# Sparse attention and a two-layer network on one core: plain chunks unit by unit with the gate in two steps, weight sums made in place, and another order of the up phase

## The chip, the cores and the metric

The program runs on one core of one Trainium2 chip. Its time is the device time of one execution in microseconds. Five engines run their own instruction queues in order and wait for one another at semaphores: TensorE (PE in the profile, its weight loads PEld), VectorE (DVE), ScalarE (ACT), GpSimd (POOL) and SyncE (SP), which issues the DMAs.

## What is computed

Attention over 8 batches, 8 heads, 576 positions with 64 elements a head; four heads see the last 32 positions, four see every 32nd. The result, as 4608 tokens of 512 elements, goes through a layer of 2048, a gate and a layer of 512, all in float32:

```python
scores = np.where(masks, scale * q @ k.T, -1e9)
attn = np.exp(scores - scores.max(-1)); attn /= attn.sum(-1) + 1e-09
x = (attn @ v).transpose(0, 2, 1, 3).reshape(4608, 512)
h = x @ w_in
g = np.where(h >= 1, h, np.where(h <= -1, 0.0, (h + 1) ** 2 / 4))
return g @ w_out
```

## The kernel before

Every product of float32 matrices is made of three fp32r matmuls, high by high, high by low and low by high, so each operand is split into a rounded high part (ACT) and the rest (DVE). The tokens go through in stages:

- **Head**: attention of batch 0.
- **Plain chunks** c = 0, 1, 2 of 512 tokens. A chunk has 16 units f of 128 hidden elements. `up(c, f)` makes h with 12 matmuls; `gate` (L620) makes the gate: `bent` and `squared` on ACT, `gated` on DVE, then the high part gh (ACT, L631; DVE in chunk 0) and the rest gl (DVE, L634); `down` (L640) adds the unit to four output banks with 12 matmuls. h has two PSUM banks in turn. In chunk 0 `down` takes one unit at a time, two units behind `up`; in chunks 1 and 2 two units at once, as soon as three are pending.
- **Super-chunks** s = 0, 1, 2 of 1024 tokens, by a Strassen scheme with 7 products in place of 8. In the up phase, `up_block` (L708), 8 pairs j of units run through 7 products m each, in the order of `UP` (L662), with 6 matmuls a product. Three accumulators belong to a pair: Y takes products 1, 6, 7 and 4, X takes 2, Z takes 5 and 3. Between the products ACT copies a bank out before the next product is added to it, DVE adds banks together, and the four gates of a pair are made. Then comes the down phase, `down_block`, with 56 products over the split gates `hl` (`prep`, L783).

The factors of the Strassen products are read from DRAM, seven ahead, into a ring of tiles (`fetch_w`). They are written there in chunks 1 and 2: `ship` (L231) writes the weights as they are, and for each of the 2 times 8 pairs a block of four **weight sums**. These are made by POOL in `recall` (L241: two adds of 512 elements, high plus low of the weights) and `combine` (L246: four adds or subtractions of 256), then split by ACT and DVE in `ship_sums` (L255) and written to DRAM as 1 MB. The attention of batches 2 to 7 runs in small steps beside all this: `START` and `LATER` give the quarter unit g at which each step stands, so its place is fixed against the products of PE. POOL also makes two steps of each softmax (L412, L436).

The order is written out by hand (`manual_schedule`); each engine works in the order of the program. h in `COMBINE` (L924) counts half units. For an entry at h, `recall` stands at h − 1, `combine` at h and `ship_sums` at h + 1, and the entries are 3 apart. All sums of chunk 1 use one room for the recalled weights and one for the sums, both in the tile xs_0 that later takes attention outputs; those of chunk 2 use rooms in w0 and w1. The outputs of a chunk leave through three `ob` buffers that attention uses as well (L652).

Of the kernel before, what the change touches and what calls it, by code (L numbers as in the profile page):

```python
# [17 lines left out]
P = 128  # L18
EPS = 1e-09
ST = 32  # L20
WR = 7
# [4 lines left out]
def tile_sparse_attention_then_ffn(  # L26
# [214 lines left out]
    def recall(i, j, w32):  # L241
        for f in range(2):
            hi, lo = (wt[2 * j + f][:, i, :, x].bitcast(F32) for x in range(2))
            nc.gpsimd.tensor_tensor(out=w32[:, 2 * f:2 * f + 2], in0=hi, in1=lo, op=ALU.add)

    def combine(i, j, w32, st):  # L246
        def block(r, c):
            return w32[:, 2 * r + c if i == 0 else 2 * c + r]

        s_ = [st[:, n, HF:] for n in range(4)]  # L250
        for to, a, b, op in ((0, block(1, 0), block(1, 1), ALU.add), (1, s_[0], block(0, 0), ALU.subtract),
                             (2, block(0, 0), block(1, 0), ALU.subtract), (3, block(0, 1), s_[1], ALU.subtract)):
            nc.gpsimd.tensor_tensor(out=s_[to], in0=a, in1=b, op=op)  # L253
# [366 lines left out]
    def gate(c, f, between=lambda: None):  # L620

        hp = o_ps.pop((c, f))
        u, gh, gl = (short(n, d, f"{a}_{c}_{f}") for n, d, a in ((6, F32, "u"), (f % 3, F32R, "gh"), (3 + f % 3, F32R, "gl")))
        bent(u, hp)
        squared(u)
        between()

        g = u if (c, f) == (0, 0) else hp
        gated(g, hp, u)
        if c:  # L630
            nc.scalar.copy(gh, g)  # L631
        else:
            nc.vector.tensor_copy(gh, g)
        nc.vector.tensor_tensor(out=gl, in0=g, in1=gh.bitcast(F32), op=ALU.subtract)  # L634
        return gh, gl
# [4 lines left out]
    def down(*units):  # L640

        c, f0, f1 = units[0][0], units[0][1], units[-1][1]
        if f0 == 0:
            o_ps[c] = [psum("o", [P, CH], f"o_{c}_{d}") for d in range(NC)]
        for d in range(NC):
            h, e = divmod(d * P, HF)
            for _, f, gs in units:
                for n, (x, y) in enumerate(HI_LO):
                    nc.tensor.matmul(o_ps[c][d], wt[f][:, 1, h, x, e:e + P], gs[y],  # L649
                                     start=f == 0 and n == 0, stop=f == NF - 1 and n == 2)  # L650
            if f1 == NF - 1:
                ob = o_p.tile([P, CH], F32, tag="ob", name=f"ob_{c}_{d}")  # L652
# [8 lines left out]
    FACTOR = {1: (0, 0), 2: (0, 1), 4: (0, 2), 5: (1, 0), 6: (1, 1), 7: (1, 2), 3: (1, 3)}  # L661
    UP = [(j - late, m) for j in range(NP + 1) for m, late in ((1, 0), (2, 0), (3, 1), (6, 0), (4, 1), (5, 0), (7, 0)) if 0 <= j - late < NP]  # L662
# [45 lines left out]
    def up_block(s, between):  # L708
        y, x, z = {}, {}, {}
        room = slot(TMP, [P, 4, CH], F32, f"tmp_{s}")  # L710
        tmp = [room[:, 2 * j % 4:2 * j % 4 + 2] for j in range(NP)]
        sets = (("b2", "b0", "b1"), ("b3", "b4", "b5"))
        for n, (j, m) in enumerate(UP):
            w_ = factor(0, j, m)
            k, jj = divmod(j, 2)
            at = sets[jj]
            if m == 1:
                y[j] = bank(at[0], [P, CH], f"y_{s}_{j}")
# [5 lines left out]
            elif m == 2:  # L724
                x[j] = bank(at[1], [P, CH], f"x_{s}_{j}")
            elif m == 5:
                z[j] = bank(at[2], [P, CH], f"z_{s}_{j}")
# [7 lines left out]
            g11, g12, g21, g22 = ga[k][:, 0, jj], ga[k][:, 1, jj], gb[k][:, 0, jj], gb[k][:, 1, jj]  # L735
            ua, ub = (tmp[j][:, i] for i in range(2))
            if m == 1:
                last = (gb[(j - 1) // 2][:, 1, (j - 1) % 2], tmp[j - 1][:, 1]) if j else None
                if last:
                    bent(last[1], last[0])  # L740
                nc.scalar.copy(g11, y[j])  # L741
                if last:
                    squared(last[1])
                    gated(last[0], *last)
            elif m == 2:
                nc.vector.tensor_tensor(out=g11, in0=x.pop(j), in1=g11, op=ALU.add)
                bent(ua, g11)
                squared(ua)
            elif m == 3:
                nc.vector.tensor_tensor(out=g12, in0=z.pop(j), in1=g12, op=ALU.add)  # L750
                bent(ub, g12)
            elif m == 6:
                nc.scalar.copy(g12, y[j])
                gated(g11, g11, ua)
                if j:
                    last = ga[(j - 1) // 2][:, 1, (j - 1) % 2], tmp[j - 1][:, 1]
                    squared(last[1])
                    gated(last[0], *last)
            elif m == 4:
                h = y.pop(j)  # L760
                bent(ua, h)
                squared(ua)
                gated(g21, h, ua)
                if jj:
                    nc.gpsimd.tensor_tensor(out=ga[k][:, 1], in0=gb[k][:, 1], in1=ga[k][:, 1], op=ALU.subtract)  # L765
            elif m == 5:
                nc.scalar.copy(g22, z[j])  # L767
            elif m == 7:
                nc.vector.tensor_tensor(out=g22, in0=y[j], in1=g22, op=ALU.add)
                if j == NP - 1:  # L770
                    bent(ub, g22)
                    squared(ub)
                    gated(g22, g22, ub)
            if j == NP - 1 and m == 3:
                squared(ub)
# [289 lines left out]
```

## Time and profile before

| | |
|---|---|
| time, median of 3 runs | 923.0 us (921.79 to 925.13) |
| the profiled execution | 923.32 us, of which 921.5 us are the span |
| PE busy | 840.6 us, 91%; mean granted clock 0.968 |
| DVE, ACT, POOL busy | 560.0, 493.9, 241.7 us |
| HBM read and written | 147.26 and 46.66 MB |

The stages in the time of the profile: head to 26.5 us, chunk 0 to 118.8, chunk 1 to about 260, chunk 2 to 393.5, then up and down phases that begin at 393.5 and 500.6 (s = 0), 588.7 and 677.3 (s = 1), 761.7 and 838.2 (s = 2). "Idle before" beside an instruction is the time in which its engine waited in front of it, and the arrow names what ended the wait. A busy engine of a stage is to be read against the stage's length, and the granted clock beside it tells whether PE's matmuls ran at full speed.

### The profile page before, as it was taken

What the parts mean: (1) busy time and instruction counts of PE and PEld (TensorE: products, weight loads), DVE (VectorE), ACT (ScalarE), POOL (GpSimd) and SP (SyncE); (2) the same over time, 40 slices, a digit from 0 to 9 for tenths busy, and PEclk for the clock granted to TensorE, in tenths of its full rate; (3) what the DMA queues carried; (4) which work ended last, traced back from release to release, by engine and by line L of the source; (5) the groups of instructions that cost most, each with busy time, mean ns of one, the idle gap of its engine ahead of it and who ended that gap; (6) DMA issues with size and microseconds to landing.
All of it is one profiled execution on the core that took longest, in us unless ns stands there. A gap on an engine that the chain in (4) does not pass through costs nothing.

```text
span 921.5 us, 17868 instructions
## 1 busy us (share of the span) xinstructions
PE 840.6 (91%) x6965; PEld 669.2 (73%) x6965; DVE 560.0 (61%) x822; ACT 493.9 (54%) x852; POOL 241.7 (26%) x244
## 2 busy tenths in 40 slices
PE   8999989859979878859999998999999899999997
PEld 6788867647768756647877786777878678887886
DVE  6899835535434453555676778567567773456665
ACT  5888833334353343436766455357764435776442
POOL 6454336646215556111223000023110000111000
PEclk9999998978989989979999999999999999999999
DMA  9908136745664765558788775678766576666664
GB/s 355 408 26 309 57 112 226 268 159 192 223 210 139 263 229 171 189 189 281 226 279 282 216 238 181 212 248 232 229 179 213 163 222 209 194 194 182 210 195 159
DMA packets 105251, 195.10 MB, mean 212 GB/s; under 512 B 17104, under 2 KB 32464, under 8 KB 104272
## 3 DMA queue, kind: packets, MB, share of 16 engines
q1 hardware_dynamic: 105168, 193.96, 65.4%
q8 instruction: 55, 0.90, 0.4%
q14 instruction: 28, 0.23, 0.1%
HBM read 147.26 MB, written 46.66 MB: 210 GB/s over the span
## 4 chain that ended last, share of the span: by engine, by line
PE 51%; DVE 20%; ACT 15%; DMA 6%; issue 4%; POOL 4%; SPq 1%; ACTq 0%; DVEq 0%; POOLq 0%
PE o L649 10%; PE y L731 9%; PE h L608 8%; PE yo L837 8%; DVE hl L700 5%; PE z L731 4%; PE xo L837 4%; ACT hl L699 3%; PE xp L509 3%; ACT tmp L612 2%; PE x L731 2%; ACT tmp L615 2%; PE sc L346 2%; POOL xs L253 2%; DVE pr L397 1%
## 5 line engine op out<-in xcount | busy, mean ns | idle before, releaser
L731 PE MATMUL y<-x,wr 128*128 128x512 f32 x576 | 144.9, 397 | 12.9 <-ACT ga L741 8.9
L649 PE MATMUL o<-gh,w 128*128 128x512 f32 x384 | 133.2, 414 | 21.7 <-ACT gh L631 21.7
L608 PE MATMUL h<-xq,w 128*128 128x512 f32 x576 | 145.5, 403 | 0.8 <-DVE xq L572 0.5
L837 PE MATMUL yo<-hl,wr 128*128 128x512 f32 x576 | 135.8, 392 | 6.5 <-DVE hl L700 5.7
L731 PEld LDWEIGHTS y<-x,wr 128*128 128x128 f32 x576 | 107.2, 189 | 39.9 <-ACT ga L741 9.3
L837 PEld LDWEIGHTS yo<-hl,wr 128*128 128x128 f32 x576 | 107.3, 188 | 33.1 <-DVE hl L700 9.2
L608 PEld LDWEIGHTS h<-xq,w 128*128 128x128 f32 x576 | 109.7, 194 | 26.2 <-DVE xq L572 1.2
L649 PEld LDWEIGHTS o<-gh,w 128*128 128x128 f32 x384 | 76.4, 199 | 40.5 <-ACT gh L631 23.8
L412 POOL TENSOR_TENSOR pr<-pr,st 128x768 f32<-128x768 f32 (+3 forms) x31 | 38.2, 1233 | 176.2 <-DVE st L408 176.0
L649 PE MATMUL o<-gl,w 128*128 128x512 f32 x192 | 79.0, 411 | 0.3 <-DVE gl L634 0.2
L837 PE MATMUL zo<-hl,wr 128*128 128x512 f32 x288 | 69.1, 394 | 7.4 <-DVE hl L700 4.5
L731 PE MATMUL z<-x,wr 128*128 128x512 f32 x288 | 74.3, 393 | 1.1 <-ACT gab L767 1.1
L837 PEld LDWEIGHTS zo<-hl,wr 128*128 128x128 f32 x288 | 53.5, 188 | 22.4 <-DVE hl L700 7.0
L436 POOL TENSOR_TENSOR pr<-pr,st 128x648 f32<-128x648 f32 (+3 forms) x30 | 35.8, 1195 | 127.2 <-DVE st L435 126.5
L765 POOL TENSOR_TENSOR ga<-gb,ga 128x1024 f32<-128x1024 f32 x9 | 21.6, 2400 | 170.3 <-DVE ga L618 163.0
L699 ACT CAST hl<-ga 128x1024 fp32r<-128x1024 f32 x36 | 37.9, 1054 | 49.3 <-DVE ga L790 22.3
L731 PEld LDWEIGHTS z<-x,wr 128*128 128x128 f32 x288 | 54.1, 189 | 13.0 <-ACT gab L767 1.5
L618 DVE SCALAR_TENSOR_TENSOR h<-h,u 128x512 f32<-128x512 f32 x47 | 32.7, 696 | 49.3 <-ACT u L615 48.9
L615 ACT ACTIVATE tmp<-tmp 128x512 f32<-128x512 f32 x96 | 60.7, 632 | 1.7
L700 DVE TENSOR_TENSOR hl<-ga,hl 128x1024 fp32r<-128x1024 f32 x36 | 45.2, 1255 | 26.1 <-ACT hl L699 26.1
L634 DVE TENSOR_TENSOR gl<-h,gh 128x512 fp32r<-128x512 f32 x47 | 32.5, 692 | 29.2 <-ACT gh L631 28.6
L612 ACT ACTIVATE u<-h,half 128x512 f32<-128x512 f32 x48 | 32.8, 684 | 31.2 <-PE h L608 31.2
(122 smaller groups left out, 1344.0 us busy)
## 6 DMA issues: line engine op xcount, KB each, us to landing
wr<-ks SPq DMA_DIRECT2D x192, 256.0 KB, 3.7
wr<-kq SPq DMA_DIRECT2D x144, 256.0 KB, 3.0
raw<-in_w SPq DMA_DIRECT2D x30, 512.0 KB, 9.6
kq<-w SPq DMA_DIRECT2D x48, 256.0 KB, 4.5
qk<-in_qk_s SPq DMA_DIRECT2D x16, 604.0 KB, 6.6
qk<-in_qk_l SPq DMA_DIRECT2D x16, 576.0 KB, 6.5
ks<-xs SPq DMA_DIRECT2D x9, 1024.0 KB, 4.9
v<-in_v_l SPq DMA_DIRECT2D x21, 384.0 KB, 6.2
```

Source lines behind the costliest of these rows:

```text
L412: eng.tensor_tensor(out=pr, in0=pr, in1=st[:, 0].unsqueeze(2).broadcast_to(list(pr.shape)), op=ALU.add)
L436: eng.tensor_tensor(out=pr, in0=pr, in1=st[:, 2].unsqueeze(2).broadcast_to(list(pr.shape)), op=ALU.mult)
L608: nc.tensor.matmul(o_ps[c, f], wt[f][:, 0, h, x, e:e + P], xq[c][:, y, cc], start=first and n == 0, stop=last and n == len(todo) - 1)
L612: nc.scalar.activation(u, h, AF.Relu, bias=half, scale=0.5)
L615: nc.scalar.activation(u, u, AF.Square)
L618: nc.vector.scalar_tensor_tensor(out=to, in0=h, scalar=1.0, in1=u, op0=ALU.max, op1=ALU.min)
L634: nc.vector.tensor_tensor(out=gl, in0=g, in1=gh.bitcast(F32), op=ALU.subtract)
L649: nc.tensor.matmul(o_ps[c][d], wt[f][:, 1, h, x, e:e + P], gs[y], start=f == 0 and n == 0, stop=f == NF - 1 and n == 2)
L699: nc.scalar.copy(t[:, 0], src)
L700: nc.vector.tensor_tensor(out=t[:, 1], in0=src, in1=t[:, 0].bitcast(F32), op=ALU.subtract)
L731: nc.tensor.matmul(to, w_[:, a, c * P:(c + 1) * P], xc[m][:, b, c], start=m in (1, 2, 5) and c + q == 0, stop=c == 1 and q == 2, skip_grou ...
L837: nc.tensor.matmul(to, w_[jj][:, a, d * P:(d + 1) * P], t[:, b, jj], start=m in (1, 2, 5) and k + jj + q == 0, stop=k == NP // 2 - 1 and j ...
```

## The change

1. **Plain chunks.** `down` takes one unit in every chunk, two units behind `up`. `gate` ends with `gated`; the split into gh and gl is a new step `rounded`. In chunk 0 it follows at once; in chunks 1 and 2 it stands after the attention steps, `ship`, `sums` and the splits of x of that half unit.
2. **Weight sums.** `recall` is gone. `combine` puts high plus low straight into the low half of the block that is shipped and makes the four sums in place, with as many POOL instructions of the same sizes. The block is one half of xs_0 (chunk 1) or xs_1 (chunk 2), in turn. `ship_sums` stands at h + 2 in place of h + 1, and the entries of `COMBINE` are 3 or 4 apart, eight to a chunk.
3. **Outputs of chunks 1 and 2** go through a room of their own with four parts (a half of xs_1, the free tile w8) in place of the three `ob` buffers.
4. **Up phase.** Product 7 is moved behind product 1 of the next pair, Y gets three banks (b2, b3, b4), X one (b0), Z two (b1, b5). The gates are cut into two halves that stand at other products; the temporaries take four rooms in turn. `prep` of the first two `hl` moves from products (7 of j = 4, 5) to (5 of j = 5, 6). `FACTOR` only follows the new order of the sums in the block.

```diff
-    def recall(i, j, w32):
+    def combine(i, j, st):
+        b = st[:, :, HF:].rearrange("p (r c) e -> p r c e", c=2)
         for f in range(2):
             hi, lo = (wt[2 * j + f][:, i, :, x].bitcast(F32) for x in range(2))
-            nc.gpsimd.tensor_tensor(out=w32[:, 2 * f:2 * f + 2], in0=hi, in1=lo, op=ALU.add)
...
+            nc.gpsimd.tensor_tensor(out=b[:, :, f] if i else b[:, f], in0=hi, in1=lo, op=ALU.add)
+        for to, x, y, op in ((3, 2, 3, ALU.add), (2, 0, 2, ALU.subtract), (0, 3, 0, ALU.subtract), (1, 1, 0, ALU.subtract)):
+            nc.gpsimd.tensor_tensor(out=st[:, to, HF:], in0=st[:, x, HF:], in1=st[:, y, HF:], op=op)
...
+    def rounded(c, f):
+        g = o_ps.pop((c, f))
+        gh, gl = (short(n + f % 3, F32R, f"{a}_{c}_{f}") for n, a in ((0, "gh"), (3, "gl")))
...
-    def down(*units):
+    def down(c, f, gs):
...
+        if f == NF - 1 and c:
+            room = x_tile(1)[:, :, :CH] if c == 1 else slot(HL_AT[0], [P, NC, CH], F32, f"ob_{c}")
...
-    UP = [(j - late, m) for j in range(NP + 1) for m, late in ((1, 0), (2, 0), (3, 1), (6, 0), (4, 1), (5, 0), (7, 0)) if 0 <= j - late < NP]
+    UP = [(j - late, m) for j in range(NP + 1) for m, late in ((1, 0), (7, 1), (2, 0), (3, 1), (6, 0), (4, 1), (5, 0)) if 0 <= j - late < NP]
...
+            before = j if m in (3, 4, 7) else j - 1
+            now = j + 1 if m in (3, 4, 7) else j
             if m == 1:
+                nc.scalar.copy(g(j, 0, 0), y[j])
+            elif m == 7:
+                added(j, 1, 1, y[j])
+                if now == NP:
+                    first_half(j, 1, 1)
             elif m == 2:
+                if before >= 0:
+                    first_half(before, 1, 1)
+                added(j, 0, 0, x.pop(j))
             elif m == 3:
+                added(j, 0, 1, z.pop(j))
+                second_half(j, 1, 1)
+                if now < NP:
+                    first_half(now, 0, 0)
+                else:
+                    first_half(j, 0, 1)
             elif m == 6:
+                nc.scalar.copy(g(j, 0, 1), y[j])
+                if before >= 0:
+                    first_half(before, 0, 1)
+                else:
+                    first_half(j, 0, 0)
+                second_half(j, 0, 0)
             elif m == 4:
+                second_half(j, 0, 1)
+                first_half(j, 1, 0, y[j])
+            if m == 5:
+                nc.scalar.copy(g(j, 1, 1), z[j])
+            if (m == 5 or m == 4 and now == NP) and before >= 0:
+                second_half(before, 1, 0, y.pop(before))
...
-        COMBINE = {3 * n: (n >= NP, n % NP) for n in range(NP + 1)} | {36 + 3 * n: (1, n) for n in range(1, NP)}
+        COMBINE = {h: (n // NP, n % NP, half) for n, (h, half) in enumerate((
+            (0, 1), (3, 0), (6, 1), (9, 0), (12, 1), (16, 1), (19, 1), (23, 1),
+            (33, 1), (36, 0), (39, 1), (42, 0), (46, 1), (50, 1), (54, 1), (58, 1)))}
...
+            for at, do in ((h, combine), (h - 2, ship_sums)):
+                if at in COMBINE:
+                    i, j, half_ = COMBINE[at]
+                    do(i, j, x_tile(at // 32)[:, :, half_ * CH:(half_ + 1) * CH])
...
-                pend.append((c, f, gate(c, f, lambda: go(mid))))
+                gate(c, f, lambda: go(mid))
+                if c == 0:
+                    pend.append((c, f, rounded(c, f)))
...
-                n = 2 if c else 1
+                if c:
+                    pend.append((c, f, rounded(c, f)))
                 if len(pend) > 2:
-                    down(*pend[:n])
-                    del pend[:n]
+                    down(*pend.pop(0))
```

`first_half(j, r, c)` is `bent` and `squared` (ACT) into the next of the four temporaries, `second_half` is `gated` (DVE), `added` is the DVE addition of a bank to the tile of that gate.

Three places show what moves. First PE in chunk 1, before; `h_1_6` is the h of unit 6, `gh_1_4` and `gl_1_4` the split gate of unit 4, `o_1_0` the first output bank.

```order
L608 MATMUL h_1_6_2323<-xq_1_148,w_6_966 128x512 x12
L649 MATMUL o_1_0_2029<-gh_1_4_2152,w_4_823 128x512
L649 MATMUL o_1_0_2029<-gl_1_4_2153,w_4_823 128x512
L649 MATMUL o_1_0_2029<-gh_1_4_2152,w_4_823 128x512
L649 MATMUL o_1_0_2029<-gh_1_5_2292,w_5_914 128x512
L649 MATMUL o_1_0_2029<-gl_1_5_2293,w_5_914 128x512
L649 MATMUL o_1_0_2029<-gh_1_5_2292,w_5_914 128x512
```

The same place of the changed program:

```order
L602 MATMUL h_1_6_2321<-xq_1_148,w_6_966 128x512 x12
L647 MATMUL o_1_0_2026<-gh_1_4_2160,w_4_823 128x512
L647 MATMUL o_1_0_2026<-gl_1_4_2161,w_4_823 128x512
L647 MATMUL o_1_0_2026<-gh_1_4_2160,w_4_823 128x512
...
L602 MATMUL h_1_7_2370<-xq_1_148,w_7_1025 128x512 x12
L647 MATMUL o_1_0_2026<-gh_1_5_2302,w_5_914 128x512
```

Behind the h of unit 6 PE took units 4 and 5 together; now it takes unit 4 alone, and unit 5 comes behind the h of unit 7.

Second, DVE at the end of chunk 2, before; `h_2_15` is the gate of the last unit, `gl_2_15` its low part, `pr` and `st` are attention's probabilities and their statistics, the L696 and L700 rows are the sums and splits of x for the first super-chunk.

```order
L618 SCALAR_TENSOR_TENSOR h_2_15_4281<-h_2_15_4281,u_2_15_4324 128x512
L634 TENSOR_TENSOR gl_2_15_4326<-h_2_15_4281,gh_2_15_4325 128x512
L423 TENSOR_REDUCE st_5_0_4224<-pr_5_0_4223 128x12
L435 RECIPROCAL st_5_0_4224<-st_5_0_4224 128x12
L397 TENSOR_TENSOR pr_5_1_4336<-sc_5_1_0_4294,m_loc_94 128x128
L397 TENSOR_TENSOR pr_5_1_4336<-sc_5_1_1_4295,m_loc_94 128x128
L397 TENSOR_TENSOR pr_5_1_4336<-sc_5_1_0_4294,m_loc_94 64x128
L397 TENSOR_TENSOR pr_5_1_4336<-sc_5_1_1_4295,m_loc_94 64x128
L408 TENSOR_REDUCE st_5_1_4337<-pr_5_1_4336 128x6
L696 TENSOR_TENSOR xs_0_1802<-xs_0_1802 128x2x512 x2
L700 TENSOR_TENSOR x_0_6_4348<-xs_0_1802,x_0_6_4348 128x1024
L700 TENSOR_TENSOR x_0_5_4351<-xs_0_1802,x_0_5_4351 128x1024
```

The same place of the changed program:

```order
L612 SCALAR_TENSOR_TENSOR h_2_15_4251<-h_2_15_4251,u_2_15_4294 128x512
L417 TENSOR_REDUCE st_5_0_4203<-pr_5_0_4202 128x12
L429 RECIPROCAL st_5_0_4203<-st_5_0_4203 128x12
L391 TENSOR_TENSOR pr_5_1_4302<-sc_5_1_0_4264,m_loc_94 128x128
L391 TENSOR_TENSOR pr_5_1_4302<-sc_5_1_1_4265,m_loc_94 128x128
L391 TENSOR_TENSOR pr_5_1_4302<-sc_5_1_0_4264,m_loc_94 64x128
L391 TENSOR_TENSOR pr_5_1_4302<-sc_5_1_1_4265,m_loc_94 64x128
L402 TENSOR_REDUCE st_5_1_4303<-pr_5_1_4302 128x6
L694 TENSOR_TENSOR xs_0_1877<-xs_0_1877 128x2x512 x2
L698 TENSOR_TENSOR x_0_6_4314<-xs_0_1877,x_0_6_4314 128x1024
L698 TENSOR_TENSOR x_0_5_4317<-xs_0_1877,x_0_5_4317 128x1024
L633 TENSOR_TENSOR gl_2_15_4321<-h_2_15_4251,gh_2_15_4320 128x512
```

`gl_2_15` moved from the row behind the gate to the end of this piece, behind the attention steps and the work on x.

Third, PE in the up phase of s = 1, before; `y_1_4` is the Y bank of pair 4, `x_1_7` the input block of product 7 (the names X and Z likewise).

```order
L731 MATMUL y_1_4_6837<-x_1_1_5903,wr_138_6722 128x512 x6
L731 MATMUL x_1_4_6855<-x_1_2_5925,wr_139_6735 128x512 x6
L731 MATMUL z_1_3_6813<-x_1_3_6145,wr_140_6751 128x512 x6
L731 MATMUL y_1_4_6837<-x_1_6_6056,wr_141_6796 128x512 x6
L731 MATMUL y_1_3_6715<-x_1_4_6283,wr_142_6808 128x512 x6
L731 MATMUL z_1_4_6910<-x_1_5_6098,wr_143_6820 128x512 x6
L731 MATMUL y_1_4_6837<-x_1_7_5989,wr_144_6834 128x512 x6
```

The same round of the changed program:

```order
L744 MATMUL y_1_4_6807<-x_1_1_5882,wr_137_6636 128x512 x6
L744 MATMUL y_1_3_6629<-x_1_7_5968,wr_138_6701 128x512 x6
L744 MATMUL x_1_4_6831<-x_1_2_5904,wr_139_6711 128x512 x6
L744 MATMUL z_1_3_6791<-x_1_3_6124,wr_140_6727 128x512 x6
L744 MATMUL y_1_4_6807<-x_1_6_6035,wr_141_6774 128x512 x6
L744 MATMUL y_1_3_6629<-x_1_4_6262,wr_142_6786 128x512 x6
L744 MATMUL z_1_4_6887<-x_1_5_6077,wr_143_6798 128x512 x6
```

Product 7 of pair 4 left the round's end, and product 7 of pair 3 stands second; between product 6 and product 7 of one pair there are now three products, before there were two.

More of the change, by code (lines that the diff above doesn't have):

```diff
@@ L620, in gate @@
     def gate(c, f, between=lambda: None):
[L622 to L623 removed]
+        hp = o_ps[c, f]
+        u = short(6, F32, f"u_{c}_{f}")
         bent(u, hp)
@@ L983, in tile_sparse_attention_then_ffn @@
             fetch_w(n)
-        down(*pend)
-        for n in range(3, WR):
-            fetch_w(n)
+        for n, a in enumerate(pend):
+            down(*a)
+            for at in range(2):
+                fetch_w(3 + 2 * n + at)
         x_steps(0, 3, 4)
```

108 lines of the change are left out of this document (32 added, 76 removed).

## The prediction

> **What bounds the kernel now.** I read the page first, then the busy times by stage, PE's waits, the chain of waits inside chunk 1, and the timelines of PE and DVE at the places where that chain crosses them. The change keeps every matmul, so only PE's waits can go, and the clock that they cost. The busy times by stage (the stretch in us, its length, then PE, PEld, DVE, ACT, POOL busy with counts, the granted clock, DMA share, GB/s) show where those lie:
>
> ```profile
> 26.50:122.00 95.50, 95.10 (x884) 76.61 (x886) 82.50 (x159) 79.89 (x159) 43.54 (x43) 1.00 0.53 194
> 122.00:265.00 143.00, 121.59 (x1193) 96.23 (x1180) 65.69 (x113) 53.88 (x100) 68.76 (x72) 0.92 0.59 199
> 265.00:405.00 140.00, 109.93 (x1117) 86.03 (x1115) 62.63 (x93) 55.82 (x104) 58.67 (x56) 0.90 0.56 190
> 588.80:681.80 93.00, 91.29 (x821) 72.64 (x820) 55.02 (x90) 61.21 (x110) 18.67 (x14) 1.00 0.78 228
> 761.80:842.00 80.20, 80.17 (x354) 66.06 (x353) 39.69 (x58) 55.10 (x91) 7.71 (x4) 1.00 0.68 198
> ```
>
> Chunk 0 (first row) and the up phases of s = 1 and 2 (last two) keep PE full at clock 1.00. Chunks 1 and 2 leave PE idle for 21 and 30 us and run it at 0.92 and 0.90, though no other engine is busy for half of the time. PE's waits say on whom:
>
> ```profile
> PE o L649 <- ACT gh L631: 21.7, 5, 6.7
> PE xp L509 <- DMA pT<-there: 9.9, 9, 4.1
> PE y L731 <- ACT ga L741: 8.9, 1, 8.9
> ```
>
> ACT makes gh late, yet it is half idle itself. The chain of waits in chunk 1 shows why; its rows from 172.35 lead to the longest of these stalls, at 188.37:
>
> ```profile
> 131.82 1.47 POOL pr L412
> ...
> 172.35 2.12 DVE xs L258
> 174.49 7.10 DMA ks<-xs
> ...
> 182.55 2.10 POOL xs L253 x3
> ...
> 185.62 0.69 ACT u L612
> 186.34 0.64 ACT u L615
> 187.00 0.71 DVE h L618
> 187.73 0.59 ACT gh L631
> ```
>
> A block of sums is split (L258) and takes 7.10 us to land in DRAM. The next `combine` (L253) overwrites the same room, so POOL waits for the landing; ACT stands at the split behind POOL, and the next unit's gate (last four rows) stands behind that in ACT's queue.
>
> **How much there is to win.** Full speed is read from two PE rows whose starts lie 24 matmuls apart, and the stretch from the first `up` of chunk 1 to the last of chunk 2 from the others:
>
> ```profile
> 118.81 2.88 PE L608 MATMUL h<-xq,w 128*128 128x512 f32 x12
> 121.62 1.17 PE L346 MATMUL sc<-qk 64*32 64x64 f32 x96
> 122.72 0.50 PE L649 MATMUL o<-gh,w 128*128 128x512 f32 x1
> ...
> 175.36 5.60 PE L608 MATMUL h<-xq,w 128*128 128x512 f32 x24
> 180.80 0.39 PE L649 MATMUL o<-gh,w 128*128 128x512 f32 x1
> ...
> 384.30 0.77 PE L346 MATMUL sc<-qk 64*32 64x64 f32 x48
> 385.00 0.50 PE L649 MATMUL o<-gh,w 128*128 128x512 f32 x1
> ```
>
> 5.44 us for 24 is 0.2267 us each. From 118.81 to 384.30 are 265.5 us with 32 `up` and 32 `down` units: 768 matmuls, 174.1 us. Attention, by starts, takes 1.10 us for 96 small matmuls (121.62 to 122.72) and 0.70 for 48 (384.30 to 385.00). A batch has eight groups of some 40 to 96; by these two rows I estimate 7.4 us for it. Three batches and one first score lie here: 23.3 us. At full speed the stretch is 197.4 us; its excess is **68 us**.
>
> What of it remains? Chunk 0 already works unit by unit, in the PE order that chunks 1 and 2 now get, with DVE and ACT busier than they will be there. A stretch at the end of chunk 1, where the last sums are through, bounds it from the other side:
>
> ```profile
> 37.79 2.88 PE L608 MATMUL h<-xq,w 128*128 128x512 f32 x12
> ...
> 225.25 4.03 PE L608 MATMUL h<-xq,w 128*128 128x512 f32 x12
> ...
> 262.17 5.60 PE L608 MATMUL h<-xq,w 128*128 128x512 f32 x24
> ```
>
> From 37.79 to 118.81 chunk 0 did 13 units of 5.44 us (70.7) and a batch of attention (7.4) in 81.0: 2.9 us of excess, 4%. From 225.25 to 262.17 chunk 1 did 132 matmuls (29.9) and three groups of attention (3.4 by the estimate) in 36.9: 3.6 us, 11%. I take 10%, **20 us** of the 197: the second stretch is the nearer one, with attention's DMA beside it, and the sums stay. The 4%, 8 us, is the lower bound.
>
> **The sums, step by step.** POOL's work stays as it is: per block two adds of 512 (L244) and four of 256 (L253).
>
> ```profile
> L244 POOL TENSOR_TENSOR xs<-w x17: 1267/1300/2289, 117.6 to 227.5; 128x512 f32<-128x512 f32 x17
> ...
> L253 POOL TENSOR_TENSOR xs<-xs 128x256 f32<-128x256 f32 x36 | 25.7, 735 | 9.2 <-DMA ks<-xs 8.4
> L257 ACT CAST xs<-xs 128x1024 fp32r<-128x1024 f32 x9 | 9.4, 1048 | 32.2 <-POOL xs L253 26.0 <-DMA pT<-there 6.1
> ```
>
> (The first row has shortest, median and longest in ns.) A block costs 2 × 1.30 + 4 × 0.74 = 5.5 us, 7.5 where both adds are slow. `ship_sums` now stands a whole unit behind it, 5.44 us and some 0.7 of attention, in place of half of that. Two halves in turn give the DMA of 7.10 us four half units (12 us) to land after a chunk's first blocks; after the later ones, where one half serves again, it has one or two (3.1 to 6.2), and there POOL will still wait. PE's deadline moves as well. Before, a gate had one `up` (2.7 us) between its h and the `down` that needs it; now two `down` and one `up`, 36 matmuls or 8.2 us. The chain in that time is the gate (0.69, 0.64, 0.71), the split of the sums (1.05, 2.12) and the low part (0.69, row below): 5.9 us. So the later seat of `rounded` hides behind 8.2 us of PE; if that cover is gone, each ship costs PE what POOL is late. One place I charge by itself: at unit 6 of chunk 2 attention writes into the half of xs_1 that has only just been shipped, and ACT waits out that DMA, about 7 us, of which I let **2 us** reach PE (0 to 5).
>
> **The end of chunk 2.** PE's last rows there, and DVE's behind the last gate:
>
> ```profile
> 385.86 0.70 DVE L618 SCALAR_TENSOR_TENSOR h<-h,u 128x512 f32<-128x512 f32 x1 [2.58 <-ACT u L615]
> 387.21 0.69 DVE L634 TENSOR_TENSOR gl<-h,gh 128x512 fp32r<-128x512 f32 x1 [0.65 <-ACT gh L631]
> 387.82 0.94 DVE L423 TENSOR_REDUCE st<-pr 128x12 f32<-128x768 f32 x1
> ...
> 393.60 2.42 DVE L700 TENSOR_TENSOR x<-xs,x 128x1024 fp32r<-128x1024 f32 x2
> ```
>
> ```profile
> 401.13 2.01 DMA out<-ob
> ```
>
> ```profile
> 139.93 0.80 PE L649 MATMUL o<-gh,w 128*128 128x512 f32 x1 [4.39 <-ACT gh L631]
> ...
> 145.09 0.82 PE L649 MATMUL o<-gh,w 128*128 128x512 f32 x2
> ...
> 412.61 2.90 PE L731 MATMUL y<-x,wr 128*128 128x512 f32 x12
> ```
>
> From 384.30 to 412.61 PE had 48 matmuls and two score groups (0.70, and 0.85 estimated), 12.4 us at full speed, and took 28.3: 15.9 of excess, most of it behind ACT's copies into `ob`, each of which waits for an output DMA of 2 us. With a room of their own those waits go. The new wait: DVE's work from 387.82 to 396.02, 8.2 us, comes ahead of the last low part, which then ends 11.3 us behind the last h. PE has 0.7 us and 24 matmuls (5.44) until then, so it stalls for 4.9. What follows such a stall is seen at 139.93: 11 matmuls to 145.09 took 5.16 us in place of 2.49, so 2.7 us more. With 0.4 for ACT's remaining copies the end has 8.0 us of excess: **8 us** saved. By the Trainium skill, page "TensorE: Matmul & The Clock Gate", section "What's actually happening", the clock is halved after an idle window of about 3.4 us and is back after about 3.4 us of work. The trace agrees on the halved speed (0.47 us a matmul) but shows it for 5.2 us; by the page the loss would be 1.7 us, an estimate, and the sum 1 us less.
>
> **The up phase.** Products 6 and 7 of a pair now have three products between them (4.1 us), before two, and Y has a third bank. The waits that this covers in s = 0 and 1, beyond the 8.9 us above:
>
> ```profile
> PE y L731 <- DVE gb L618: 2.2, 3, 0.8
> PE y L731 <- ACT ga L753: 0.9, 2, 0.6
> ```
>
> **3 us** saved. s = 2 is full already, and the last round keeps its order (7, 3, 4), so the down phase starts as before. `prep` of the second `hl` moves by some six products and still stands ten (13.6 us) ahead of the down phase; the conversion hides there.
>
> **The sum.** 68 − 20 − 2 = 46 us in the chunks, 8 at their end, 3 in the up phase: 57. From the profiled execution's 923.3 us, which stands 0.3 above the median, that gives **866 us**.
>
> **Rivals.** First, *POOL becomes the bound of the chunks.* A block may queue behind two softmax steps of 1.47 us and so be 4 us late for its split; after PE's slack of 8.2 − 5.9 us, PE sees up to 1.7 us, and more where attention's DVE steps eat the slack. At 1.5 us for each of 16 blocks: 24 us, **890**. For: POOL is busy 127 us in the two chunks, 64% of 197. Against: in the chain above it waited and did not work. By the Trainium skill, page "GPSIMD Engine Reference", section "Specifications", POOL shares its SBUF access with DVE and contends with DVE instructions that have two SBUF inputs. The trace agrees (1267 to 2289 ns for one form), and denser chunks would make more adds slow ones.
>
> Second, *attention's DMA takes the place.* From spread to values a step has 7 quarter units: 14.5 us at the chunks' old pace (265.5 us for 128 quarters), 12 at the new. Nine such gathers stand in the chunks; at 2.5 us each, **888**. For: PE waited 9.9 us for pT even so. Against: s = 1 runs its 56 quarters in 88.6 us, 1.6 each, at DMA share 0.78, and PE lists no wait for pT there.
>
> Third, *the change doesn't do what it says*: if the landings were not what held POOL, half of the chunks' gain stays away, **889**. For: POOL's waits for landings are 8.4 us in chunk 1 against 26.0 us that ACT waits for POOL. Against: the longer way to the split serves the rest.
>
> Fourth, on the other side, *the up phase's new order chains ACT and DVE.* Half of each gate waits for DVE's addition, as it does now at times (between 383 and 450):
>
> ```profile
> ACT tmp L612 <- DVE ga L746: 5.8, 4, 1.7
> ```
>
> With two such waits of 1.45 us reaching PE in each of the 24 rounds: 70 us, **936**. From 2.4 us a round on it outweighs the gain. Against: each bank gets 4.1 us where 2.7 left s = 2 without a wait.
>
> **How the numbers follow.** Forecast 866 (849 to 880): 0.62. POOL: 0.16. Attention's DMA: 0.09. Half of the gain: 0.08. The up phase, slower: 0.03. No change within 0.3%, which is about what a measurement of this kernel can tell: 0.02. With 2 in 10 left out the range reaches from 849 (chunk 0's 4%, nothing at xs_1, 3 us more in the up phase of s = 0) to 895, past the three cases near 890. Faster by over 0.3%: 0.95.
>
> **What will show it.** Right: a granted clock of 0.97 or more in chunks 1 and 2, the stretch from the first to the last `up` at about 220 us; ACT's waits for `combine` under 15 us; one stall of 4 to 6 us at the last unit of chunk 2; no wait for `ob`. Wrong: ACT still waiting 3 us and more for POOL at each split, PE waiting for pT at every gather, or waits of 1 us and more in every round of s = 2.

## The result and the profile after

The changed kernel takes **893.6 us** (median of 4 runs, 891.9 to 896.6) beside 924.1 us (921.8 to 926.0) for the kernel before on the same chip: ratio 0.967, 95% interval 0.964 to 0.971. It is faster and inside the range of 849 to 895, but 27.6 us slower than the predicted 866 and outside the 849 to 880 that the prediction gave to its own account; the range reached so far only because of the rivals near 890. The busy times by stage of the changed kernel (columns as in the prediction: stretch, length, PE, PEld, DVE, ACT, POOL with counts, granted clock, DMA share, GB/s) say where those are:

```profile
26.50:122.00 95.50, 95.08 (x884) 76.61 (x885) 82.48 (x160) 79.80 (x159) 40.97 (x41) 1.00 0.53 196
122.00:250.00 128.00, 113.89 (x1165) 90.92 (x1152) 61.99 (x109) 51.04 (x95) 64.36 (x67) 0.92 0.64 212
250.00:388.00 138.00, 116.94 (x1141) 92.52 (x1139) 62.96 (x97) 56.61 (x106) 58.87 (x62) 0.90 0.60 203
565.40:651.65 86.25, 85.46 (x801) 69.62 (x800) 51.31 (x88) 60.20 (x106) 17.43 (x13) 1.00 0.78 236
```

Chunk 0 and the up phase (first and last row) are full at clock 1.00. Chunks 1 and 2 (second and third) still have PE idle for 14 and 21 us, and their clock is the same 0.92 and 0.90. PE's longest wait in them before (118 to 385; us in total, times, longest) was this:

```profile
PE o L649 <- ACT gh L631: 20.5, 4, 6.7
```

In the changed kernel these are the five largest:

```profile
PE sc L340 <- ACT xs L557: 9.9, 5, 3.7
PE sc L340 <- DVE xq L566: 6.8, 3, 4.1
PE xp L503 <- DMA pT<-there: 5.6, 6, 1.4
PE o L647 <- ACT gh L630: 4.7, 1, 4.7
PE o L647 <- ACT ob L651: 4.0, 2, 3.8
```

Of the 20.5 us of waits for gh one of 4.7 us is left. In their place the scores of the next attention group (`sc`) wait longer for ACT and DVE to copy the last group's results (L557, L566) out of their bank: 16.7 us, beside 10.5 before. Who holds ACT and POOL up there (118 to 370), before:

```profile
ACT xs L257 <- POOL xs L253: 26.0, 6, 8.3
ACT st L257 <- POOL st L253: 16.7, 5, 6.6
```

```profile
POOL st L253 <- DMA ks<-st: 15.0, 4, 4.8
POOL xs L253 <- DMA ks<-xs: 8.4, 2, 4.9
POOL xs L244 <- ACT xs L563: 7.2, 1, 7.2
```

And in the changed kernel:

```profile
ACT xs L251 <- POOL xs L247: 26.0, 10, 5.4
ACT xs L557 <- DMA ks<-xs: 20.6, 5, 6.0
...
POOL xs L245 <- DMA ks<-xs: 20.1, 4, 7.0
POOL xs L245 <- ACT xs L557: 16.4, 2, 8.3
```

Two things stand side by side. ACT waits 26.0 us at the split (L251) for POOL's `combine`; before the change this was 42.7 in the same window (26.0 for the first token tile, 16.7 for the weight slots). And POOL's waits at the room of the sums did not go, they grew from 30.6 to 36.5 us: attention's copies and POOL wait for each other and for landings, since both write into the token tile in which the blocks of sums lie. All six of POOL's waits stand ahead of a block that takes the same half as the block before it (entries 16, 19, 23, 50, 54 and 58 of `COMBINE`): the halves take turns only for the first blocks of a chunk. The chain of waits of the changed kernel shows the second (start, length, what):

```profile
338.33 5.13 DMA ks<-xs
...
343.48 0.50 ACT xs L557
...
344.05 2.55 POOL xs L245 x2
...
349.89 1.06 ACT xs L251
...
352.23 5.44 DMA ks<-xs
...
357.74 0.93 ACT xs L557 x7
...
358.72 1.51 PE sc L340 x88
```

A block lands (338.33 to 343.46), only then can ACT copy attention's output into that tile, only then can POOL start the next block there, and 5.4 us of its landing stand ahead of the next copy, for which PE waits.

POOL's lateness takes the same way. At unit 6 of chunk 2, the place that the prediction charged by itself, ACT's timeline shows (start, length, instruction, idle time ahead of it and what ended it):

```profile
300.86 1.04 ACT L251 CAST xs<-xs 128x1024 fp32r<-128x1024 f32 x1 [3.71 <-POOL xs L247]
...
308.63 0.71 ACT L557 COPY xs<-xp 128x128 f32<-128x128 f32 x3 [5.97 <-DMA ks<-xs]
```

And PE's:

```profile
308.95 1.98 PE L340 MATMUL sc<-qk 64*64 64x54 f32 x40 [3.72 <-ACT xs L557]
```

The split waited 3.71 us for POOL, so its block went off late (303.18), and the copy for which PE waits stood behind that landing.

Two stretches, worked out as in the prediction. From 118.82 to the end of the last `up` at 369.52 are 250.7 us; 31 `down` units lie in it now, so full speed is 197.4 − 2.7 = 194.7 and the excess is 56 us; before it was 68. **So the chunks gave 12 us where 46 were forecast.** The end of chunk 2 is this (PE's timeline; start, length, instruction, idle time ahead of it and what ended it):

```profile
369.52 0.77 PE L340 MATMUL sc<-qk 64*32 64x64 f32 x48
...
380.70 0.80 PE L647 MATMUL o<-gh,w 128*128 128x512 f32 x1 [4.73 <-ACT gh L630]
382.19 0.79 PE L647 MATMUL o<-gl,w 128*128 128x512 f32 x1 [0.70 <-DVE gl L633]
...
393.78 2.45 PE L744 MATMUL y<-x,wr 128*128 128x512 f32 x10
```

From 369.52 to 393.78 are 24.3 us, with 60 matmuls (13.6) and 1.55 of scores in them: 9.1 of excess, where 8.0 were forecast (before it was 15.9). From there to the end of the span are 498.8 us; before (412.61 to 921.5) 508.9: 10 us where 3 were forecast.

### The profile page after: what moved, and what is told of

The parts are those of the page before. It is cut to its first block, busy times and chain, and to the rows that moved or that the text cites. A ratio compares the mean times of both kernels' runs of the same rounds, so it can differ in the third digit from the quotient of the medians.

```text
span 892.6 us, 17867 instructions
## 1 busy us (share of the span) xinstructions
PE 833.7 (93%) x6965; PEld 669.8 (75%) x6965; DVE 553.7 (62%) x822; ACT 496.7 (56%) x852; POOL 233.9 (26%) x244
## 4 chain that ended last, share of the span: by engine, by line
PE 55%; DVE 15%; ACT 9%; DMA 9%; POOL 7%; issue 3%; SPq 1%; ACTq 0%; DVEq 0%; POOLq 0%
PE y L744 12%; PE yo L845 10%; PE o L647 8%; PE h L602 7%; PE z L744 6%; DVE hl L698 5%; PE xo L845 4%; DMA ks<-xs 4%; ACT hl L697 3%; PE x L744 3%; POOL xs L247 3%; POOL xs L245 3%; PE sc L340 2%; PE xp L503 2%; DMA qk<-in_qk_s 1%
## 5 line engine op out<-in xcount | busy, mean ns | idle before, releaser
L602 PE MATMUL h<-xq,w 128*128 128x512 f32 x576 | 147.9, 407 | 3.0 <-DVE gl L633 2.1
L647 PE MATMUL o<-gh,w 128*128 128x512 f32 x384 | 136.2, 417 | 8.7 <-ACT gh L630 4.7
L744 PE MATMUL y<-x,wr 128*128 128x512 f32 x576 | 141.7, 392 | 0.3 <-ACT ga L752 0.3
L602 PEld LDWEIGHTS h<-xq,w 128*128 128x128 f32 x576 | 111.7, 197 | 29.7 <-DVE gl L633 3.0
L845 PEld LDWEIGHTS zo<-hl,wr 128*128 128x128 f32 x288 | 53.5, 188 | 22.1 <-DVE hl L698 7.0
L698 DVE TENSOR_TENSOR hl<-ga,hl 128x1024 fp32r<-128x1024 f32 x36 | 44.8, 1245 | 33.0 <-ACT hl L697 33.0
L697 ACT CAST hl<-ga 128x1024 fp32r<-128x1024 f32 x36 | 38.0, 1057 | 49.0 <-DVE ga L798 22.1
L340 PE MATMUL sc<-qk 64*32 64x64 f32 (+1 forms) x1856 | 34.5, 232 | 19.8 <-ACT xs L557 9.9
```

The costliest lines, as they stand in the source:

```text
L340: nc.tensor.matmul(sc[j][i * Q:(i + 1) * Q, s, p], qk[:, 0, q0:q0 + Q], qk[:, 1, k0:k0 + W], start=u not in covered, stop=u not in covered)
L602: nc.tensor.matmul(o_ps[c, f], wt[f][:, 0, h, x, e:e + P], xq[c][:, y, cc], start=first and n == 0, stop=last and n == len(todo) - 1)
L697: nc.scalar.copy(t[:, 0], src)
L698: nc.vector.tensor_tensor(out=t[:, 1], in0=src, in1=t[:, 0].bitcast(F32), op=ALU.subtract)
L744: nc.tensor.matmul(to, w_[:, a, c * P:(c + 1) * P], xc[m][:, b, c], start=m in (1, 2, 5) and c + q == 0, stop=c == 1 and q == 2, skip_grou ...
L845: nc.tensor.matmul(to, w_[jj][:, a, d * P:(d + 1) * P], t[:, b, jj], start=m in (1, 2, 5) and k + jj + q == 0, stop=k == NP // 2 - 1 and j ...
```

## The experiments

Each ratio is to runs of the kernel before beside it on the same chip (medians of 922.1 to 925.2 us); "saved" is (1 − ratio) × 923, taken before the ratio is rounded. e5 and e9 leave out part of the sums and only bound what these cost; the others compute all of it.

| run | us | ratio, 95% interval | saved |
|---|---|---|---|
| the change | 893.6 | 0.967 (0.964 to 0.971) | 30 |
| e1, before with the up phase alone | 914.9 | 0.989 (0.987 to 0.990) | 11 |
| e2, before with the units' part alone | 903.5 | 0.976 (0.974 to 0.978) | 22 |
| e3, before with the sums alone | 923.5 | 0.999 (0.997 to 1.001) | 1 |
| e4, change, six blocks in other rooms | 881.4 | 0.953 (0.949 to 0.956) | 44 |
| e5, change, one block in place of 16 | 853.8 | 0.925 (0.921 to 0.928) | 70 |
| e6, e3 with e4's rooms | 915.8 | 0.993 (0.990 to 0.995) | 7 |
| e7, change, rounding put back | 909.6 | 0.986 (0.982 to 0.990) | 13 |
| e8, change, seats apart | 870.9 | 0.944 (0.940 to 0.949) | 52 |
| e9, change, POOL's differences left out | 869.6 | 0.941 (0.940 to 0.943) | 54 |
| e10, before with the two steps alone | 909.0 | 0.986 (0.984 to 0.988) | 13 |
| e11, e8 with other seats and order | 880.2 | 0.954 (0.952 to 0.956) | 43 |
| e12, e11, ship one half unit later | 865.9 | 0.938 (0.936 to 0.941) | 57 |

**One part at a time.** e1 takes the new `UP` and `up_block`; e2 takes `gate`, `rounded`, `down` with its rooms and the loops that call them; e3 takes `combine`, the table `COMBINE` with `sums`, and the `FACTOR` that goes with them.

> The kernel before with the new up phase alone (order of products, halves of the gates, three Y banks); the sums, the pairs of units and the down products stay as before. The prediction's term for this part is -3, so 921 beside 924. The two traces, stage against stage, show 10 us less in the six up and down stages together (85.3 after 88.0, 86.3 after 88.1, 86.3 after 88.6, 82.8 after 84.4, 76.2 after 76.5, 82.0 after 83.3); if all of that belongs to this part, 914. If it comes instead from what the first two parts leave behind in the queues, this run stays at 921 to 924.

> The kernel before with the first part alone: plain chunks unit by unit, gates in two steps, results of chunks 1 and 2 in a room for all four blocks. The prediction's term for the end of chunk 2 is -8, and 6.8 us is what the traces show there. Theory A (what holds the chunks up lies in the sums and their room): 917, within 2. Theory B (the pairs of units held the chunks up as well): below 913, since most of the 12 us saved in the chunks would come with this part.

> The kernel before with the sums alone: in place, spread, and in halves of the tile that later holds the next tokens; the units still go in pairs. The prediction's term is -46, so 878. The traces show only 12 us less in the stretch from chunk 1's first product to the last `up` of chunk 2. Theory A (that gain is the sums' own): 912, within 3. Theory B (the gain needs units one by one, since with pairs each combine still stands between two units): 918 or more. If the new rooms, which attention's outputs share, are a loss for the old order: 924 or more.

e1 comes out where all of the stages' gain belongs to the up phase, e2 as theory B has it, and e3 with no gain, as its theory B allows. The three save 11, 22 and 1, together 34 beside 30 for all: they add up within the intervals. The order of sizes is the reverse of the forecast: the sums, priced at 46, are worth nothing by themselves, and the units' part, priced at 8, is worth 22. The chunks show the same: from the first `up` of chunk 1 to the start of chunk 2's last `up` matmul e2 takes 247.7 us (120.50 to 368.2) and the change 250.4 (118.82 to 369.2), so the sums added nothing there to what the units' part gave.

**The shared tile.** e4 and e6 move the blocks from h = 39 on:

```diff
-                    do(i, j, x_tile(at // 32)[:, :, half_ * CH:(half_ + 1) * CH])
+                    do(i, j, block_at(at, half_))
...
+            if at < 39:
+                return x_tile(at // 32)[:, :, half_ * CH:(half_ + 1) * CH]
+            if at not in blocks:
+                blocks[at] = slot(("w0", "w1")[len(blocks) % 2], [P, 4, CH], F32, f"st_{at}")
+            return blocks[at]
```

> The changed kernel with one difference: the six blocks of sums from the third one of chunk 2 on lie in two weight slots that are free by then, in turn, and no longer in the halves of the tile that attention writes. Theory A (what the chunks still lose, 56 us over the pace of the matmuls, is lost where attention's outputs and the sums share a tile and wait for each other and for the block's way to memory): chunk 2's share of it is about half, and its last quarter, now at a granted clock of 0.89 with 9 us without a matmul, is the worst; 8 to 14 us less, 880 to 886. Theory B (POOL is simply late with 5.6 us of work on each block, wherever it lies): no change, 892 to 895. Theory C (waits for pieces of attention fetched from memory set the pace): no change either, and the waits of the `xp` products for `pT` stay at 6.6 us.

> The kernel before with the sums alone (in place and spread, the units still in pairs), and with the six blocks from the third one of chunk 2 on in two weight slots in turn. It is the run with the sums alone, 923.5, with the shared tile taken away in chunk 2. Theory A (the new sums were worth something all along, and the shared tile ate it): 12 less, as it was in the changed kernel, 910 to 913. Theory B (with pairs PE waits for ACT's gh anyway, so that a free room is worth nothing): 918 to 924.

e4 saves 14 more than the change, as theory A has it. ACT's waits in e4 (118 to 370):

```profile
ACT xs L251 <- POOL xs L247: 16.1, 6, 4.7
ACT st L251 <- POOL st L247: 15.6, 4, 5.1
...
ACT xs L557 <- DMA ks<-xs: 6.3, 2, 4.9
```

Attention's waits for landings fell from 20.6 to 6.3 us; the waits at the split, 31.7 for both rooms, did not fall, so it was the room and not POOL's pace that these 14 us were lost to. e6 saves 6 more than e3, less than half of that and between the two theories: with pairs part of the gain is covered. PE's waits for gh, 8.9 us in e3 and 8.4 in e6, may be what covers it; no run shows that.

**What the sums cost at all, and POOL's share.** e5 leaves out 15 of the 16 blocks; e9 leaves out the loop of four differences in `combine` (L247).

```diff
-        for to, x, y, op in ((3, 2, 3, ALU.add), (2, 0, 2, ALU.subtract), (0, 3, 0, ALU.subtract), (1, 1, 0, ALU.subtract)):
-            nc.gpsimd.tensor_tensor(out=st[:, to, HF:], in0=st[:, x, HF:], in1=st[:, y, HF:], op=op)
```

> The changed kernel with 15 of the 16 blocks of sums left out: the first block is made and shipped, and the up and down phases read it in place of the others. This bounds what the sums still cost. Theory A (nearly all that the chunks lose over the matmuls' pace is lost behind the sums): the chunks' excess falls to the 10 per cent that the prediction took from the end of chunk 1, some 35 us less than the changed kernel, 858 to 864. Theory B (once the rooms are apart, attention's own chain and the clock hold the rest): about the time with the six blocks in weight slots, 881, or a few us below, not under 872.

> The changed kernel with the four differences of each block left out (L247), so that POOL has two instructions for a block in place of six, 2.6 us in place of 5.6; the blocks' seats, halves, splits and transfers stay as they are. With 15 blocks gone 40 us went, with the seats taken apart some 15 of these. Theory A (what is lost is lost over the shared halves and the landings): 885 to 892, since POOL then waits where it worked. Theory B (POOL's own work makes the splits late, the prediction's first rival, priced at 24 us): 868 to 878.

e5 saves 40 more than the change: theory A, and beyond it. Its stretch from the first `up` of chunk 1 (118.24) to the end of chunk 2's last (330.29) is 212.1 us against 194.7: 17 of excess, 9%. e9 saves **24** more than the change, theory B; it still writes every block to DRAM, so these are not the transfers' cost. ACT's waits in it (118 to 370; line numbers are two lower from the split on):

```profile
ACT xs L555 <- DMA ks<-xs: 19.4, 6, 5.5
...
ACT xs L249 <- POOL xs L245: 3.9, 5, 1.5
```

And POOL's in the same run:

```profile
POOL xs L245 <- ACT xs L555: 17.7, 2, 9.6
POOL xs L245 <- DMA ks<-xs: 16.1, 4, 5.8
```

The waits of the shared tile are those of the change, 19.4 beside 20.6 and 33.8 beside 36.5 us; only ACT's wait at the split is gone, 3.9 beside 26.0. So 24 us hang on POOL's own 3 us a block. With e4's 14 that makes 38 of the 40 that the sums cost the changed kernel. No run makes both edits, and the place at 300.86 has both causes in one stall, so that the two sizes add up so well may be chance. PE's waits for attention's copies fell from 16.7 to 9.2 us in e9 and those for pT from 5.6 to 0.6, 12.5 in all. Most of the rest goes with the clock: from 180 to 243 it is 0.92 in the change and 1.00 in e9.

**The gate's two steps.** e7 puts the rounding back right behind the gate in the changed kernel; e10 takes only the new seat of the rounding into the kernel before.

```diff
                 gate(c, f, lambda: go(mid))
-                if c == 0:
-                    pend.append((c, f, rounded(c, f)))
+                pend.append((c, f, rounded(c, f)))
...
-                if c:
-                    pend.append((c, f, rounded(c, f)))
                 if len(pend) > 2:
```

> The changed kernel with `rounded` put back right behind `gate` in chunks 1 and 2, ahead of attention's steps and the sums; units still go one by one. Theory A (what the first part gains comes from `down` being two units behind its gate, not from the gate's two steps): no loss, 889 to 894, and at the end of chunk 2 a gain of up to 5 us, since the last low part no longer stands behind the x steps. Theory B (rounding behind attention's steps is what keeps ACT and DVE from standing at the gate): 898 or more.

> The kernel before with one edit: in chunks 1 and 2 the gate's rounding into gh and gl (`rounded`) stands behind attention's steps and the sums; units in pairs, old sums, old up phase. With the rounding put back ahead of them the changed kernel lost 16 of the 22 us that the first part is worth by itself. Theory A (the two steps are worth that by themselves): 906 to 911. Theory B (they are worth it only when `down` comes two units later, since in pairs the second unit's gh is needed at once): 922 or more, because gh then comes later still; up to 930.

e7 loses 17, theory B, and e10 saves 13, theory A: the seat of the rounding is worth that with pairs and without them. In e7 ACT waits 22.1 us at gh for the gate's last step on DVE, as it did in the kernel before (24.1 in 28 waits; 3.5 in the change), and attention's copies stand behind that. ACT's row of e7's waits:

```profile
ACT gh L630 <- DVE h L612: 22.1, 27, 1.3
```

And PE's row of them:

```profile
PE sc L340 <- ACT xs L557: 18.0, 4, 8.4
```

PE waits 18.0 us for those copies, beside 9.9 in the change. The second half of e7's theory A holds all the same: the end of chunk 2, from the start of the last `up` matmul to that of the first z product, takes 20.4 us, beside 23.1 in the change. In e10 the reverse is seen, since the last rounding stands behind the x steps and the pair waits for it (PE's timeline):

```profile
378.39 0.79 PE L654 MATMUL o<-gh,w 128*128 128x512 f32 x1 [7.97 <-ACT gh L636]
```

So e10's end takes 27.9 us, beside 26.6 in the kernel before (both with 48 matmuls), and its 13 is what the chunks gain less that. e2 has both the seat and units one by one, and its end takes 22.0 with 60 matmuls.

**A version that uses what was found.** e8 puts seven blocks of chunk 2 into weight slots that are free by then, seven blocks into chunk 1, chunk 0's results into a half of the first token tile, and the last unit's rounding ahead of the x steps. e11 puts ten blocks into chunk 2, nine of them in weight slots, and ships the blocks in another order. Its main edits against the change are below; e12 is e11 with one number changed, 3 in place of 2 in the `h - 2` of `sums`, and the piece shows e12:

```diff
-            (0, 1), (3, 0), (6, 1), (9, 0), (12, 1), (16, 1), (19, 1), (23, 1),
-            (33, 1), (36, 0), (39, 1), (42, 0), (46, 1), (50, 1), (54, 1), (58, 1)))}
+            (0, 0), (4, 0), (7, 1), (10, 0), (13, 1), (24, 1),
+            (33, 1), (37, "w0"), (40, "w1"), (43, "w2"), (45, "w3"), (48, "w4"), (50, "w5"), (53, "w6"), (55, "w0"), (58, "w1")))}
...
-            for at, do in ((h, combine), (h - 2, ship_sums)):
+            for at, do in ((h, combine), (h - 3, ship_sums)):
...
+                last = (c, f) == (CLASSIC - 1, NF - 1)
+                if c == 0 or last:
+                    pend.append((c, f, rounded(c, f)))
```

> The changed kernel with every shared seat that the traces name taken apart: nine blocks in chunk 2, seven of these in weight slots that are free by then (four slots in turn), seven blocks in chunk 1, alternating between the halves as far as attention allows; chunk 0's results in a half of the first token tile in place of three small buffers; and the last unit's rounding ahead of the x steps. From 881.4 with the six blocks moved: 4.7 + 2.7 us for the last unit's stall and its clock, 3.8 + 1 for chunk 0's results, and for the sums of chunk 1, which in that run still make ACT wait 16 us for POOL and POOL 15 us for landings, up to 10. Theory A (the shared rooms are what is left): 862 to 872. Theory B (attention's chain and the clock): 874 to 878, the two stalls alone.

> The kernel with the seats taken apart (870.9), with six blocks in chunk 1 in place of seven and ten in chunk 2, eight of these in seven weight slots that are free by then. In the run before it PE stood 7.7 us at 194.8 behind an attention copy that waited for the landing of chunk 1's last block in the same half: that block is gone from there. Theory A (that stall and its clock): 860 to 865. Theory B (ten blocks with POOL's 5.6 us each make chunk 2 late in turn): 870 to 875.

> The run with more seats, and each block shipped three half units behind its combine in place of two, so that ACT's and DVE's split stands less behind POOL. Theory A (POOL's lateness still holds ACT, 15 us of waits in the run with the seats apart): 3 to 8 us less than the run beside it. Theory B (those waits are off PE's path once a gate has two units of slack): within 2 us of it.

e8 saves 22 more than the change, in theory A's range. Its longest stall is the shared tile once more. The chain of waits ahead of it, from the landing of a block on:

```profile
188.66 5.08 DMA ks<-xs
...
193.83 0.34 ACT xs L557
```

And PE's row behind it:

```profile
194.78 2.15 PE L340 MATMUL sc<-qk 64*32 64x64 f32 x96 [7.73 <-DVE xq L566]
```

e11 took that block away and yet was 9 us slower than e8; neither theory had that, and no run took its edits apart. e12 is **14 us faster than e11** by the later ship alone, more than its theory A had, and at 865.9 us the fastest version that leaves nothing out: ratio 0.938, the interval clear of the change's. ACT's waits for POOL at the split in e11:

```profile
ACT xs L251 <- POOL xs L247: 11.1, 4, 3.9
...
ACT st L251 <- POOL st L247: 6.9, 2, 5.3
```

The same in e12:

```profile
ACT xs L251 <- POOL xs L247: 2.7, 3, 1.5
ACT st L251 <- POOL st L247: 2.1, 2, 1.6
```

18.0 us became 4.8. POOL's work is no shorter; its lateness costs little when nobody stands behind it in order. The later ship was not tried on the changed kernel by itself.

## Why the prediction was off, step by step

The direction and the range came out right, the sum did not, and part of the agreement is luck: 34 us that the chunks did not give were offset by 7 more than forecast from the up and down phases, and what brought 893.6 into the range was the room left for rivals near 890. Of the prediction's marks of being right, the stall at the last unit came true (4.73 us); the clock (0.92 and 0.90 for 0.97 or more), the stretch of the chunks (250.7 us for about 220) and ACT's waits for `combine` (26.0 us for under 15) did not.

**The chunks: 46 forecast, 12 found. The step that failed is "I take 10%, 20 us of the 197 … and the sums stay".** The 10% was read where the last sums of chunk 1 were through, and that is what it is worth: without the sums the excess is 9% (e5). With them it is 56 us. Two prices were missing.
- *POOL's own lateness, 24 us (e9).* The prediction let the two `down` units and one `up` behind a gate, 8.2 us, hide the split, and put "each ship costs PE what POOL is late" at nothing. The cover holds for gh alone: behind the split in ACT's queue stand attention's copies, behind the late landing too, and PE's next scores wait for those. The first rival had POOL's lateness with 24 us and 890 in all, near the 893.6 measured, but by another way, through gh and PE's slack there; that the size agrees is luck in part. What was held against it, that POOL "waited and did not work" in one chain of the kernel before, spoke of that chain alone.
- *The shared tile, 14 us (e4), priced at 2.* The prediction looked at one place, unit 6 of chunk 2, and saw rightly that ACT would wait out a landing: 5.97 us, of which 3.72 reached PE, and twelve matmuls behind it took 4.53 us in place of 2.72. It is five places, 20.6 us, and POOL waits in turn. That POOL would still wait where one half serves again the prediction said itself, and put at nothing; these are the six waits of 36.5 us.

**What the chunks did gain was put down to the wrong part.** The sums alone save nothing (e3). The rounding's later seat saves 13 to 17 (e7, e10); the prediction used it only as a longer deadline and did not see that ACT's standing at gh (24.1 us before, 3.5 in the change) held attention's copies.

**The end of chunk 2: right.** Forecast 8.0 us of excess with a new stall of 4.9; measured 9.1 with 4.73, and 0.70 more for the low part. The 4.73 are for gh, which stands behind the splits of x on ACT; the prediction had the stall at the low part on DVE. The waits for `ob` are gone there. At the start of chunk 1 there is a new one, which the prediction put at nothing: chunk 0's four results still share three buffers, ACT waits 4.6 us for one to leave, and PE stands 3.84 us at 141.97, about where the kernel before stood 4.39 for gh.

**The up phase: right in kind, 3 forecast, 11 saved (e1).** PE's listed waits for Y's bank were the 3. What was mis-sized is "the down phase starts as before". PE's row for `hl` behind 400 us in the kernel before:

```profile
PE yo L837 <- DVE hl L700: 5.7, 9, 1.1
```

And in e1:

```profile
PE yo L847 <- DVE hl L700: 3.6, 7, 0.5
```

The waits at the start of the down phases went with the others. All listed waits behind 400, but for the 8.9 us at the first round, fell from 19.2 to 14.3; e1's time from the first z product to the end fell by 8.1. The 3 us between lie in no listed wait, and where they went was not tried; the clock was 1.00 in these stages before as well, but for the last one's 0.99.

**The other rivals.** Attention's DMA did not become the limit: 5.6 us of waits for pT, beside 9.0. The third rival, at 889, holds in part: with 36.5 us of waits for its room in place of 30.6, the change did not free POOL; e9's 24 us are POOL's own work and come on top of those waits. The up phase's order chained nothing.

## What to carry to other kernels

A queue that runs in order lends its slack to whatever is next in it: before pricing a late producer at nothing, list everything that stands behind the waiting instruction, and who waits for that, rather than only the deadline the change was made for. In e12 putting the consumer later (one half unit, 14 us) took away most of ACT's waits (18.0 to 4.8), as shortening the producer did in e9 (26.0 to 3.9). And a free corner of a tile that another stream will write is a queue of its own; take the full list of that stream's writes in the time, not one of them.

## What the runs showed of the hardware

**The clock.** It falls behind stalls shorter than the 4.39 us that the prediction used. In e5 a stall of 3.18 us, with one of 0.70 behind the first matmul, went with a granted clock of 0.50 from 338.90 to 345.72; its matmuls took some 0.43 us:

```profile
339.91 0.80 PE L649 MATMUL o<-gh,w 128*128 128x512 f32 x1 [3.18 <-ACT gh L632]
```

In the changed kernel two stalls of 1.39 and 0.76 us, 0.3 us of work between them, were followed by twelve matmuls in 4.2 us in place of 2.7, the clock at 0.50 for 3.41 us:

```profile
333.28 0.33 PE L503 MATMUL xp<-pT,v 54*64 54x64 f32 x4 [1.39 <-DMA pT<-there]
334.37 1.09 PE L503 MATMUL xp<-pT,v 54*64 54x64 f32 x44 [0.76 <-DMA pT<-there]
335.39 4.40 PE L602 MATMUL h<-xq,w 128*128 128x512 f32 x12
```

```profile
334.95:338.36 3.41, 3.41 (x27) 2.71 (x19) 1.28 (x2) 2.36 (x3) 0.94 (x2) 0.50 0.20 76
```

(The last row is the busy time by stretch, with the granted clock third from its end.) A stall of 1.40 us by itself went without: the twelve matmuls behind it took 2.94 us.

```profile
258.06 3.01 PE L602 MATMUL h<-xq,w 128*128 128x512 f32 x12 [1.40 <-DVE gl L633]
```

Between 118 and 370 the changed kernel's trace has nine stretches at 0.50, six of 3.41 us and three of 6.83. At 0.50 these 41 us cost up to half of themselves; the listed waits ahead of 369.52 sum to 29.6 us. The two make up most of the 56 us of excess.

**POOL's adds.** An add of 128x512 in `combine` takes about 1.29 us or about 2.28, hardly anything between. In the kernel before 11 of 32 are slow, in the change 2, in e12 6 and in e8 8. At the start of each slow one DVE was at work on a split of a block (L252; L258 before) or of x (L698; L700 before); adds that had already begun when such a split started stayed fast, and the split could then take longer (2.06 us beside 1.23). POOL's busy time in all went from 241.7 to 233.9 us.
